# Moving one exp and two value mixing bursts in a fused attention and feed-forward kernel

## The chip, the cores and the metric

The kernel runs on one core of a Trainium2 chip. The metric is the device time of one execution in microseconds; the median of three runs of the kernel before is 246.46 us. A core has TensorE (matrix products into PSUM), VectorE, ScalarE and GpSimd, and queues that issue DMAs; here SyncE issues the outputs and the transposing DMAs, GpSimd the loads.

## The reference

Attention within blocks, where the blocks of keys and values are first mixed by a doubly normalised matrix, and then a gated feed-forward step over all 3072 tokens:

```python
# q, k, v: (4, 8, 768, 64); sort_net: (4, 8, 8, 8); weights 512x1536, 512x1536, 1536x512
P = sort_net
for _ in range(5):
    P = exp(P - max(P, -1)); P = P / (sum(P, -1) + 1e-9); P = P / (sum(P, -2) + 1e-9)
k_sorted = einsum('bhij,bhjcd->bhicd', P, k_b)      # blocks of 96 rows
v_sorted = einsum('bhij,bhjcd->bhicd', P, v_b)
attn = softmax(q_b @ k_sorted.T / 8)                # within each block
x = attn @ v_sorted                                 # as (3072, 512)
g = x @ w_gate
out = (g / (1 + exp(-g)) * (x @ w_val)) @ w_out
```

## The kernel before

After a start-up that computes `P` and the first attention units by hand, the work is written as eight feed-forward passes, `ffn(0)` to `ffn(7)`; the text calls them the first to the eighth pass. Pass `n` takes 384 tokens (half of a batch). It runs 12 steps `m`; each is a `gate` (four matmuls of 128x384, line 410), the tanh on ScalarE (line 418), `gs` on VectorE (line 420), a `value` (four matmuls, line 428) and `h` on VectorE (line 433). `gate` and `value` write to a ring of three PSUM banks ("gen"), so that the third bank after one comes back to it: a `gate` or `value` waits until `gs` or `h` has read what stood there. Between the steps lie the three output steps of the pass before, `outp(n - 1, t3, part)`: three parts of four matmuls (line 445) and, with the last, the copy `o_sb` on ScalarE (line 450) and a DMA from SyncE. In the second pass the output steps come after the steps m = 7, 9 and 11, in the later ones after 3, 7 and 11.

Into these passes `merge` puts the attention of the batches to come. Each side item has a due time; the main items have costs (0.65 for a `gate` or a `value`, 0.87 for an output part), and an item is put behind the first main item at whose end the summed cost has reached its due time. TensorE, GpSimd and ScalarE keep the order in which the program is written; VectorE's order is a planner's.

Attention comes in pairs of units. `scores` writes a unit's scores to one of two wide PSUM tiles, "b" for the first and "a" for the second unit of a pair; `exps` is the exp on ScalarE (line 345); `av` multiplies with the mixed values (line 359), VectorE divides (`r_sb`, line 363, and `st`, line 365), and `x_dma` lets SyncE transpose `st` into `xt`, the next pass's input (line 391). Each of the four `xt` slices of a pass is read by one of a `gate`'s four matmuls. A mixing burst takes the same two wide tiles: `kq_chunk` (keys, line 269) and `v_pair_chunk` (values of batches 2 and 3, line 310) fill "b", which VectorE copies out (line 247), then "a", which ScalarE copies out (line 249). The next burst cannot write a tile before its copy has ended. The values come over `vch`, which GpSimd lays out from a load that a one-element copy, `hold` (line 639), delays until the third pass's input has landed.

Of the kernel before, what the change touches and what calls it, by code (L numbers as in the profile page):

```python
# [17 lines left out]
def kernel(  # L18
# [226 lines left out]
    def drain(eng, dst, src):  # L245
        if eng == "v":
            nc.vector.tensor_copy(dst, src)  # L247
        else:
            nc.scalar.copy(dst, src)  # L249
# [13 lines left out]
    def kq_chunk(b, at, n, eng, tag):  # L263
        dst = kqt_tile(b)[:, 0:2 * GI * C].rearrange("p (n c) -> p n c", c=C)
        rm = rmix[b].rearrange("p a (g two) i -> p two (a g) i", two=2)
        tp = chunk_tile("tkq", n // 8, tag).rearrange("p (l n) -> p l n", n=2 * GI)
        for lc in range(n):
            for two in range(2):
                nc.tensor.matmul(tp[two * D:(two + 1) * D, lc, :],  # L269
                                 lhsT=kq_at(b, at + lc),  # L270
                                 rhs=rm[:, two], start=True, stop=True)
        drain(eng, dst[:, :, at:at + n], tp.transpose([0, 2, 1]))
# [31 lines left out]
    def v_pair_chunk(pair, at, n, eng, tag):  # L304
        dst = vt_tile(pair)[:, :, :, at:at + n]
        tp = chunk_tile("tv", n // 4, tag).rearrange("p (u l n) -> p u l n", u=2, n=H * NB)
        for ld in range(n):
            col = (at + ld) * C
            for u, rows in enumerate((lowr, highr)):
                nc.tensor.matmul(tp[:, u, ld, :], lhsT=vch[rows, col:col + 128],  # L310
                                 rhs=rmix["p"][rows, u].rearrange("p a b -> p (a b)"),
                                 start=True, stop=True)
        drain(eng, dst, tp[0:C].transpose([0, 1, 3, 2]))
# [4 lines left out]
    def scores(b, u, tag):  # L318
        half, g = divmod(u, H2)
        k_sb, k_at, q_sb, q_at = ((kqts[b], 0, kqts[b], GI * C) if b < 2 else  # L320
                                  (kqts["p"], (b - 2) * GI * C, kqts["q"], (b - 2) * GI * C))
        if tag == "gen":
            wide = None
            pss = [bank_tile("qk"), bank_tile("qk")]
        else:
            wide = pair_tile("qk", tag).rearrange("p (two n) -> p two n", two=2)
            pss = [wide[:, 0], wide[:, 1]]
        for i4 in range(4):
            at = (g * NB + half * 4 + i4) * C
            for two in range(2):  # L330
                lo = two * D
                nc.tensor.matmul(pss[two][:, i4 * C:(i4 + 1) * C],  # L332
                                 lhsT=k_sb[lo:lo + D, k_at + at:k_at + at + 128],
                                 rhs=q_sb[lo:lo + D, q_at + at:q_at + at + C],
                                 start=True, stop=True)
        return wide, pss

    def exps(b, u, wide, pss):
        n = ecount[0] % 8
        ecount[0] += 2  # L340
        if wide is None:
            for two in range(2):
                nc.scalar.activation(e_all[:, n + two, 0:4 * C], pss[two][0:C, 0:4 * C], AF.Exp, scale=scale)
        else:
            nc.scalar.activation(e_all[:, n:n + 2, 0:4 * C], wide[0:C, :, 0:4 * C], AF.Exp, scale=scale)  # L345
        es[(b, u)] = [e_all[:, n, :], e_all[:, n + 1, :]]

    def qk(b, u, tag="b"):
        exps(b, u, *scores(b, u, tag))

    def av(b, u, tag="a"):
        half, g = divmod(u, H2)
        vt = vts[b // 2][:, b % 2].rearrange("p (h i) e -> p h i e", h=H)
        av_ps = pair_tile("av_ps", tag).rearrange("p (two n) -> p two n", two=2)
        o = av_ps.rearrange("p two (i e) -> p two i e", i=4)
        for two in range(2):
            e = es[(b, u)][two]
            for i4 in range(4):
                nc.tensor.matmul(o[:, two, i4, 0:D + 1], lhsT=e[:, i4 * C:i4 * C + 128],  # L359
                                 rhs=vt[:, 2 * g + two, half * 4 + i4, 0:D + 1],  # L360
                                 start=True, stop=True)
        r_sb = ssp.tile([C, 2, 4, 1], FP32, name="r_sb", tag="r")
        nc.vector.reciprocal(r_sb, o[0:C, :, :, D:D + 1])  # L363
        st = ssp.tile([C, 4, 2, D], BF16, name="st", tag="st")
        nc.vector.tensor_tensor(st.rearrange("p i two d -> p two i d"), o[0:C, :, :, 0:D],  # L365
                                r_sb.to_broadcast([C, 2, 4, D]), op=ALU.mult)
        sts[(b, u)] = st
# [11 lines left out]
    def xtr(b, u):  # L379
        half, g = divmod(u, H2)  # L380
        if g == 0:
            xts[(b, half)] = xtp.tile([128, H2, TW], BF16, name=f"xt{b}_{half}", tag="xt")
        x_ps = xt_tile("x", 1)[:, 0]
        x_to(x_ps, b, u)
        return xts[(b, half)][:, g, :], x_ps.rearrange("p a b -> p (a b)")

    def x_dma(b, u):
        half, g = divmod(u, H2)
        if g == 0:
            xts[(b, half)] = xtp.tile([128, H2, TW], BF16, name=f"xt{b}_{half}", tag="xt")  # L390
        nc.sync.dma_start_transpose(out=xts[(b, half)][:, g, :].rearrange("p (i c) -> p i c", c=C),
                                    in_=sts.pop((b, u)).rearrange("p i two d -> p (i two d)"))
# [176 lines left out]
    man = tc.manual_schedule(engines={ET.PE, ET.Pool, ET.Activation})  # L569
    man.__enter__()  # L570

    def units(b, us, ats, avs=(1.9, 3.6), lag=3.1):
        us = list(us)
        todo = []
        for n, at in enumerate(ats):
            u, u2 = us[2 * n:2 * n + 2]
            held = []
            todo.append((at, lambda u=u, u2=u2, held=held: (qk(b, u, "b"), held.append(scores(b, u2, "a")))))
            todo.append((at + 1.3, lambda u2=u2, held=held: exps(b, u2, *held[0])))
            for w, tag, t in ((u, "b", avs[0]), (u2, "a", avs[1])):  # L580
                if b == 0:
                    todo.append((at + t, lambda w=w, tag=tag: av(b, w, tag)))
                    todo.append((at + t + lag, lambda w=w: drain("v", *xtr(b, w))))
                else:
                    todo.append((at + t, lambda w=w, tag=tag: (av(b, w, tag), x_dma(b, w))))
        return todo

    def kqs(b, ats):
        return [(at, lambda n=n: (kq_chunk(b, n * 32, 16, "v", "b"), kq_chunk(b, n * 32 + 16, 16, "s", "a")))
                for n, at in enumerate(ats)]  # L590
# [4 lines left out]
    def v_pairs(ats):  # L595
        return [(at, lambda m=m: (v_pair_chunk(1, m * 16, 8, "v", "b"), v_pair_chunk(1, m * 16 + 8, 8, "s", "a")))
                for m, at in ats]

    def merge(main, side):
        done, k = 0.0, 0  # L600
        side = sorted(side, key=lambda t: t[0])
        for c, f in main:
            f()
            done += c
            while k < len(side) and side[k][0] <= done:
                side[k][1]()
                k += 1
        while k < len(side):
            side[k][1]()
            k += 1  # L610

    def ffn(n):
        todo = []
        for m in range(NFC):
            if n > 0 or m > 1:
                todo.append((0.65, lambda m=m: gate(n, m)))
            if n > 0 or m > 0:
                todo.append((0.65, lambda m=m: value(n, m)))
            ends = (7, 9, 11) if n == 1 else (3, 7, 11)
            if n > 0 and m in ends:  # L620
                for part in range(3):
                    todo.append((0.87, lambda t3=ends.index(m), part=part: outp(n - 1, t3, part)))
        return todo
# [7 lines left out]
    def q0_rest():  # L631
        q0_chunk(1, 0, 16, "s", "b")
        q0_chunk(1, 16, 8, "v", "a")

    merge(ffn(0), [(0.0, q0_rest)] + units(0, range(4, 8), (2.0, 6.6)))
    merge(ffn(1), kqs(1, (0.6, 3.3, 7.1)) + vs(v_chunk, 16, (5.2, 5.8, 8.4, 9.1))
          + units(1, range(4), (11.0, 15.6), (1.3, 2.6)))
    hold = const.tile([1, 1], BF16)
    nc.gpsimd.tensor_copy(hold, xts[(1, 0)][0:1, H2 - 1, 0:1])
    load_v(2, 0, 4)  # L640
# [1 line left out]
    for s in range(4):  # L642
        copy_v(nc.gpsimd, 1, both, s)
    nc.vector.memset(kqt_tile("p")[:, 2 * GI * C:], 0.0)
    merge(ffn(2), units(1, range(4, 8), (0.0, 5.5)) + kqs("p", (13.0, 14.7, 20.7)) + v_pairs([(0, 22.5)])
          + [(13.0, lambda: q_dma(2)), (16.4, lambda: q_dma(3))])
    merge(ffn(3), v_pairs([(1, 0.0), (2, 5.1), (3, 6.9)]) + units(2, range(4), (9.8, 14.9)))
    merge(ffn(4), units(2, range(4, 8), (0.0, 8.0)))
    merge(ffn(5), units(3, range(4), (0.0, 8.0)))
    merge(ffn(6), units(3, range(4, 8), (0.0, 8.0)))  # L650
# [36 lines left out]
```

## Time and profile before

| | |
|---|---|
| median of three runs | 246.46 us (246.25 to 246.61) |
| profiled execution | 246.0 us, span 244.2 us |
| TensorE busy | 237.1 us, 97% |
| VectorE busy | 154.8 us, 63% |
| ScalarE busy | 112.3 us, 46% |
| GpSimd busy | 51.3 us, 21% |
| DMA | 24.77 MB, mean 101 GB/s |
| granted TensorE clock | 1.0 |

The span is the time from the first to the last event that the profiler saw; the profiled execution's own time is 1.8 us longer. Lines such as L410 are those of the kernel before. The chain of waits follows the work back from the last instruction, at each step to what released it. "issue" is time in which an engine waited for nothing that the profile shows. PEld is TensorE's loading of weights, which overlaps its matmuls, and SPq is SyncE's queue of DMAs. Where a row has a time and a length, the first number is the start in us from the span's start, the second the length; the modelled ends of matmuls overlap the next ones by a little.

### The profile page before, as it was taken

The numbers are of one execution on the slowest core, as the hardware profiler recorded it, in microseconds if no ns is written. First come the engines' busy times: TensorE is split into PE (matmuls) and PEld (weight loads), VectorE is DVE, ScalarE is ACT, GpSimd is POOL, SyncE is SP. The second block draws the span as 40 slices with busy tenths as digits, with TensorE's granted clock in tenths as the row PEclk, the third lists the DMA queues.
The fourth block names the chain that finished last, engine by engine and source line by source line (L and its number), as shares of the span: only waits on it lengthen the run. The fifth ranks groups of instructions, "written<-read, shape, count | busy, mean of one in ns | idle before, by whom it ended". The sixth has DMA issues, their size and how long they took to land.

```text
span 244.2 us, 6162 instructions
## 1 busy us (share of the span) xinstructions
PE 237.1 (97%) x2617; PEld 139.4 (57%) x2617; DVE 154.8 (63%) x326; ACT 112.3 (46%) x189; POOL 51.3 (21%) x45
## 2 busy tenths in 40 slices
PE   7799999999999999999999999999999999999994
PEld 6375666676455565555555555565556555555543
DVE  6786789876664685777755845674675576445700
ACT  3977554467435435365543452254325334332312
POOL 5992139990002059200000000000000000000000
PEclk9999999999999999999999999999999999999999
DMA  5989999999996999410121212012111211110122
GB/s 99 215 129 208 206 213 213 204 214 190 161 137 139 190 162 159 119 43 3 46 75 32 62 59 71 8 59 63 32 43 46 75 36 43 43 43 3 43 86 86
DMA packets 39642, 24.77 MB, mean 101 GB/s; under 512 B 29376, under 2 KB 34368, under 8 KB 39616
## 3 DMA queue, kind: packets, MB, share of 16 engines
q0 software_dynamic: 19632, 14.16, 38.9%
q1 hardware_dynamic: 19840, 10.17, 17.0%
q8 instruction: 20, 0.33, 0.6%
q10 hardware_dynamic: 144, 0.07, 0.1%
q14 instruction: 6, 0.05, 0.1%
HBM read 28.32 MB, written 7.86 MB: 148 GB/s over the span
## 4 chain that ended last, share of the span: by engine, by line
PE 90%; DVE 4%; DMA 2%; ACT 1%; issue 1%; POOLq 0%
PE v_ps L428 25%; PE o_ps L445 25%; PE g_ps L410 25%; PE av_ps L359 3%; PE qk L332 3%; PE tkq L269 3%; DMA v<-in_v_dram 2%; PE o_ps L461 1%; PE idle_ps L477 1%; PE tv L300 1%; DVE st L365 1%; DVE vt L247 1%; PE tq L279 1%; PE tv L310 1%; PE g_ps L550 1%
## 5 line engine op out<-in xcount | busy, mean ns | idle before, releaser
L420 DVE SCALAR_TENSOR_TENSOR gs_sb<-th_sb,g_ps 128x384 bf16<-128x384 bf16 x96 | 52.9, 551 | 52.4 <-ACT th_sb L418 49.6
L428 PE MATMUL v_ps<-xt,wv_sb 128*128 128x384 bf16 x380 | 77.3, 326 | 0.0
L410 PE MATMUL g_ps<-xt,wg_sb 128*128 128x384 bf16 x376 | 76.6, 325 | 0.2
L418 ACT ACTIVATE th_sb<-g_ps 128x384 bf16<-128x384 f32 x96 | 47.1, 491 | 55.5 <-PE g_ps L410 52.7
L445 PE MATMUL o_ps<-wo,h 128*128 128x512 bf16 x276 | 64.2, 379 | 0.0
L433 DVE SCALAR_TENSOR_TENSOR h<-v_ps,gs_sb 128x384 bf16<-128x384 f32 x96 | 53.4, 556 | 7.6 <-PE tkq L269 0.5
L428 PEld LDWEIGHTS <-wv_sb 128*128 128x128 bf16 x380 | 35.3, 97 | 23.2 <-issue 0.2
L410 PEld LDWEIGHTS <-wg_sb 128*128 128x128 bf16 x376 | 34.9, 97 | 23.7 <-issue 0.4
L445 PEld LDWEIGHTS <-h 128*128 128x128 bf16 x276 | 26.1, 98 | 28.7
L450 ACT COPY o_sb<-o_ps 128x512 f32<-128x512 f32 x23 | 13.5, 586 | 49.0 <-PE o_ps L445 49.0
L148 POOL COPY vch<-v 64x1536 bf16<-64x1536 bf16 (+2 forms) x11 | 28.8, 2657 | 13.0 <-DMA v<-in_v_dram 12.9
L345 ACT ACTIVATE e_all<-qk 96x768 bf16<-96x768 f32 x30 | 23.3, 801 | 4.5 <-PE qk L332 4.5
L365 DVE TENSOR_TENSOR st<-av_ps,r_sb 96x512 bf16<-96x512 f32 x32 | 21.8, 680 | 0.3
L359 PEld LDWEIGHTS <-e_all 96*128 96x128 bf16 x256 | 11.8, 97 | 6.0 <-ACT e_all L345 1.7
L359 PE MATMUL av_ps<-vt,e_all 96*128 96x65 bf16 x256 | 13.1, 193 | 0.5 <-ACT e_all L345 0.5
L249 ACT CAST vt<-tv 96x1024 bf16<-96x1024 f32 (+1 forms) x11 | 10.1, 931 | 4.7 <-PE tv L310 3.6
L363 DVE RECIPROCAL r_sb<-av_ps 96x8 f32<-96x8 f32 x32 | 6.4, 199 | 8.7 <-PE av_ps L359 8.7
L247 DVE CAST vt<-tv 96x1024 bf16<-96x1024 f32 (+1 forms) x7 | 7.4, 1064 | 2.2 <-PE tv L310 1.7
L477 PE MATMUL idle_ps<-warm_sb 128*128 128x512 bf16 x25 | 7.6, 411 | 0.0
L247 DVE COPY oq_v<-o_ps 128x128 f32<-128x128 f32 x1 | 0.3, 292 | 9.3 <-PE o_ps L461 9.3
L395 POOL DMA_DIRECT2D q_scr<-in_q_dram x2 | 5.6, 3178 | 0.0
L146 ACT COPY vch<-v 64x768 bf16<-64x768 bf16 (+1 forms) x4 | 5.4, 1384 | 0.2 <-DMA v<-in_v_dram 0.2
(83 smaller groups left out, 129.8 us busy)
## 6 DMA issues: line engine op xcount, KB each, us to landing
out_dram<-o_sb SPq DMA_DIRECT2D x23, 256.0 KB, 2.0
v<-in_v_dram POOLq DMA_DIRECT2D x4, 384.0 KB, 12.6
wg_sb<-in_moe_w_gate_dram POOLq DMA_DIRECT2D x3, 512.0 KB, 11.2
wv_sb<-in_moe_w_val_dram POOLq DMA_DIRECT2D x3, 512.0 KB, 13.0
wo<-in_moe_w_out_dram POOLq DMA_DIRECT2D x3, 512.0 KB, 16.2
kqp<-in_k_dram POOLq DMA_DIRECT2D x2, 768.0 KB, 10.1
q_scr<-in_q_dram POOLq DMA_DIRECT2D x2, 768.0 KB, 18.8
v<-in_v_dram POOLq DMA_DIRECT2D x2, 768.0 KB, 9.8
```

The source lines that it names most:

```text
L148: eng.tensor_copy(dst, src.transpose([0, 2, 1]))
L247: nc.vector.tensor_copy(dst, src)
L345: nc.scalar.activation(e_all[:, n:n + 2, 0:4 * C], wide[0:C, :, 0:4 * C], AF.Exp, scale=scale)
L359: nc.tensor.matmul(o[:, two, i4, 0:D + 1], lhsT=e[:, i4 * C:i4 * C + 128], rhs=vt[:, 2 * g + two, half * 4 + i4, 0:D + 1], start=True, sto ...
L365: nc.vector.tensor_tensor(st.rearrange("p i two d -> p two i d"), o[0:C, :, :, 0:D], r_sb.to_broadcast([C, 2, 4, D]), op=ALU.mult)
L410: nc.tensor.matmul(g_ps, lhsT=wg_sb[:, kc, ts(m, 128)], rhs=xt[:, kc, :], start=(kc == 0), stop=(kc == NKC - 1))
L418: nc.scalar.activation(th_sb, g_ps, AF.Tanh, scale=0.5)
L420: nc.vector.scalar_tensor_tensor(gs_sb, th_sb, 1.0, g_ps, op0=ALU.add, op1=ALU.mult)
L428: nc.tensor.matmul(v_ps, lhsT=wv_sb[:, kc, ts(m, 128)], rhs=xt[:, kc, :], start=(kc == 0), stop=(kc == NKC - 1))
L433: nc.vector.scalar_tensor_tensor(h_tiles[n][:, m, :], v_ps, 0.5, gs_tiles.pop(m), op0=ALU.mult, op1=ALU.mult)
L445: nc.tensor.matmul(o_ps, lhsT=h_w[:, m, ts(t3, 128)], rhs=wo_sb[part][:, m % 4, :], start=(m == 0), stop=(m == NFC - 1))
L450: nc.scalar.copy(o_sb, o_ps)
```

## The change

`units` gets a parameter for the time between a pair's scores and its second exp; it was 1.3 and stays so everywhere but in the second pass, where it is 0.9. In the third pass the first value mixing burst is due at 21.6 instead of 22.5, and the second, which was the first side item of the fourth pass, is due at 22.5 in the third.

```diff
-    def units(b, us, ats, avs=(1.9, 3.6), lag=3.1):
+    def units(b, us, ats, avs=(1.9, 3.6), lag=3.1, second=1.3):
...
             todo.append((at, lambda u=u, u2=u2, held=held: (qk(b, u, "b"), held.append(scores(b, u2, "a")))))
-            todo.append((at + 1.3, lambda u2=u2, held=held: exps(b, u2, *held[0])))
+            todo.append((at + second, lambda u2=u2, held=held: exps(b, u2, *held[0])))
...
     merge(ffn(1), kqs(1, (0.6, 3.3, 7.1)) + vs(v_chunk, 16, (5.2, 5.8, 8.4, 9.1))
-          + units(1, range(4), (11.0, 15.6), (1.3, 2.6)))
+          + units(1, range(4), (11.0, 15.6), (1.3, 2.6), second=0.9))
...
-    merge(ffn(2), units(1, range(4, 8), (0.0, 5.5)) + kqs("p", (13.0, 14.7, 20.7)) + v_pairs([(0, 22.5)])
+    merge(ffn(2), units(1, range(4, 8), (0.0, 5.5)) + kqs("p", (13.0, 14.7, 20.7)) + v_pairs([(0, 21.6), (1, 22.5)])
           + [(13.0, lambda: q_dma(2)), (16.4, lambda: q_dma(3))])
-    merge(ffn(3), v_pairs([(1, 0.0), (2, 5.1), (3, 6.9)]) + units(2, range(4), (9.8, 14.9)))
+    merge(ffn(3), v_pairs([(2, 5.1), (3, 6.9)]) + units(2, range(4), (9.8, 14.9)))
```

On ScalarE the second exp of the second pass's first pair comes to stand ahead of the copy of the first output step. On TensorE the last output step of the third pass reads: last key burst, part one, first value burst, part two, second value burst, part three, and then the fourth pass's first `gate`; before, it read key burst, parts one and two, first value burst, part three, `gate`, second value burst, `value`. The order on SyncE and GpSimd is the same in both kernels.

## Prediction

> **What bounds the kernel.** I read the page first (busy times, then the chain of waits), then the table of waits of TensorE, then the chain and the timeline in the two stretches that the diff touches, and last the times to landing of the DMAs that those stretches start.
>
> ```profile
> PE 237.1 (97%) x2617; PEld 139.4 (57%) x2617; DVE 154.8 (63%) x326; ACT 112.3 (46%) x189; POOL 51.3 (21%) x45
> PE 90%; DVE 4%; DMA 2%; ACT 1%; issue 1%; POOLq 0%
> PE av_ps L359 <- ACT e_all L345: 0.5, 1, 0.5
> ```
>
> TensorE is busy 97% of the span and is 90% of the chain that ended last. After the start-up it waits by name for another engine once in the whole run: 0.5 us for an exp. A change of order can therefore gain only where TensorE stands still, and costs wherever it makes TensorE stand still anew. The named wait lies in the second pass (chain of waits, that stretch; start, us, what):
>
> ```profile
> 62.38 0.26 PE av_ps L359 x8
> 62.90 0.82 ACT e_all L345
> 63.76 0.42 PE av_ps L359 x8
> 64.18 0.65 PE v_ps L428 x4
> ```
>
> TensorE's timeline gives `gate` at 62.46 and the next `value` at 64.02; between them stands the second `av` of the pair, held until ScalarE has finished its exp. ScalarE's rows there are: exp of the first unit 60.42 to 61.23, idle 1.19, copy `o_sb` 62.42 to 63.01, exp of the second unit 62.90 to 63.71. The second exp had its scores long before: it stood behind a copy that itself waited for TensorE.
>
> The other stretch is the seam between the third and fourth pass (timeline; idle time before an instruction in brackets):
>
> ```profile
> 101.56 1.22 DVE L247 CAST kqtp<-tkq 128x1024 bf16<-128x1024 f32 x1
> 101.61 1.90 PE L445 MATMUL o_ps<-wo,h 128*128 128x512 bf16 x8
> 103.44 0.64 PE L310 MATMUL tv<-rmixp,vch 64*128 64x64 bf16 x32
> 103.89 1.22 DVE L247 CAST vt<-tv 96x1024 bf16<-96x1024 f32 x1 [1.11 <-PE tv L310]
> 104.12 1.01 ACT L249 CAST vt<-tv 96x1024 bf16<-96x1024 f32 x1 [1.39 <-PE tv L310]
> 105.64 0.64 PE L310 MATMUL tv<-rmixp,vch 64*128 64x64 bf16 x32
> 106.73 1.21 DVE L247 CAST vt<-tv 96x1024 bf16<-96x1024 f32 x1
> 107.87 0.54 DVE L433 SCALAR_TENSOR_TENSOR h<-v_ps,gs_sb 128x384 bf16<-128x384 f32 x1
> 108.46 0.81 PE L410 MATMUL g_ps<-xt,wg_sb 128*128 128x384 bf16 x4
> ```
>
> The first mixing burst (103.44) finds its PSUM tile long free. The second (105.64) sends a cast to VectorE ahead of `h`; `h` ends at 108.41, and the `gate` that needs the bank it frees starts at 108.46 instead of 108.17 (0.65 after the `value` at 107.52). That is a hold of 0.29 us which the table of waits does not name.
>
> **Edit 1, the exp.** In the second pass the first pair's second exp now stands right behind the first exp, ahead of the copy. For the second pair of that pass the new due time (16.5 instead of 16.9) falls behind the same output part as before, so nothing moves there. No instruction is added. The two exps run as one stretch of 1.50 us (the second pair's row at 66.45), so the second ends at about 61.9, before the copy's data is there at 62.4: the copy costs nothing more, it lies in the idle 1.19. The `av` then starts as the matching place in the third pass does (`gate` 84.46, `value`, then `av` 85.76 and `gate` 86.01): 0.65 for the `gate`, 0.25 for the `av`. From `gate` to `value` that is 0.90 instead of 64.02 - 62.46 = 1.56. **Gain 0.66, taken as 0.65** (the start of the `av` moves from 63.76 to 63.11).
>
> What is late next: VectorE now does reciprocal, `gs`, `st`, `h` from 63.6 on, by the spacing of its rows at 64.12 to 65.43 ending `h` at about 65.6; the output step that takes the bank of that `value` comes at 66.51 - 0.65 = 65.86, so 0.3 remains. SyncE's transposes of this unit and the two later ones are issued earlier by the same shift; the queue order of SyncE and GpSimd does not change.
>
> **Edit 2, the bursts.** Of the third pass's last output step (three parts of four matmuls), the first burst moves from behind part two to behind part one, the second from behind the next pass's first `gate` to behind part two. TensorE's work is the same; four changes between burst and other work before, four after. The cover of each PSUM drain shrinks. Step by step, in the old times:
> - The drain of the last key burst ends at 101.56 + 1.22 = 102.78. Part one starts at 101.61 and is over for the next burst after about 0.96 (half of 1.83, plus the change), 102.57. First burst at 102.82: **held 0.25**.
> - From a burst's start to its VectorE cast 0.45 (103.44 to 103.89), cast 1.22, release 0.04: 1.71. Under it lie the burst (0.57, 103.44 to 104.02) and one part (0.96): 1.53. Second burst at 104.53: **held 0.18**.
> - Second burst 0.57, part three 0.87 (104.02 to 104.89): first `gate` at 105.97. ScalarE's casts (1.01 each, 0.68 behind the bursts) end at 106.22, when the copy of the output wants to start anyway. From first to third `gate` an undisturbed pass takes 2.64 (95.12 to 97.76): third `gate` at 108.61 instead of 108.46.
>
> **Sum of edit 2: 0.15 later, taken as 0.14** (the next burst at 111.19 comes out 0.14 later): the hold of 0.29 and its side effects go, 0.43 come. Bounds: below, -0.29, if only the old hold goes and both drains happen to end in time; above, +0.54, if the key drain ends as late after its burst as the first key burst's (90.14 to 92.85, 2.71 instead of 2.31, 0.40 more). I take the middle rows, since they are those of this very place.
>
> **Total: -0.65 + 0.14 = -0.51.** The profiled execution took 246.0 (span 244.2 and 1.8 around it), so 245.5 for it; its time is 0.46 below the median of the runs, 246.46. On the median: 245.95. A measurement of this kernel can tell about 0.2%, 0.49 us, from no change: the forecast lies on that edge.
>
> **A rule against it.** The four transposes that make the next pass's input are on their way while GpSimd's cast of q still occupies the DMA engines; to landing they take 7.7, 7.1, 3.9 and 2.3 us (issues at 63.62, 66.05, 69.65, 72.61), faster as that traffic ends. The fourth lands by 74.99, when GpSimd's `hold` copy that waits for it runs; the `gate` at 74.83 needs it for its fourth matmul, at 75.32. So 0.33 of cover is all there is.
> The Trainium skill, DMA: Bandwidth & Descriptors, section "Issuing engines are not separate DMA queues", says that DMAs of different issuing engines share the same 16 engines and interleave; read strictly, issuing earlier only queues earlier, and the sum would be that of rival B below.
>
> A second one: TensorE's granted clock stayed at 1.00 through both holds (windows of 2 and 10 us; TensorE's busy time first).
>
> ```profile
> 62.00:64.00 2.00, 1.51 (x22) 0.87 (x21) 0.89 (x2) 1.58 (x3) 0.00 (x0) 1.00 2.48 157
> 100.00:110.00 10.00, 9.87 (x170) 5.76 (x168) 7.14 (x11) 5.44 (x8) 0.00 (x0) 1.00 0.12 47
> ```
>
> The Trainium skill, TensorE: Matmul & The Clock Gate, section "A second HAM failure mode: psum-queue depth-cycling", warns that short idles while PSUM banks are cycled can throttle the clock; one 3.4 us window at half clock, an estimate from that page, would make the total about +1.2. The 0.65 hold above did not do it, so I give that no place in the sum.
>
> **Rivals.**
> - **B, the fourth transpose does not move.** The output DMA ahead of it on SyncE took 1.68 us to issue (70.87) where others take 0.33 to 0.54, as if held by what was still under way. If its landing stays at 74.99 while the matmul wants it at 74.67, TensorE waits 0.32: -0.51 + 0.32 = -0.19, 246.27. Against it: all that the fourth transpose waits for (its `st`, the output copy) moves with TensorE.
> - **C, slower.** The fourth transpose meets more of the q traffic and takes 3.9 like the third: issued at 71.96 it lands at 75.86, 1.19 after its matmul wants it: -0.51 + 1.19 = +0.68, 247.14. It decides against the change from a landing of 3.7 on (a wait of 1.0). Against it: at 72 to 73 us the DMA share was down to 0.06.
> - **D, the bursts cost nothing.** -0.65 - 0.29 = -0.94, 245.52. For it: VectorE is better placed after the seam, with both casts out of the way of `gs` and `h`. Against it: the drain of 1.22 is longer than one part.
> - That the exp does not change its place is excluded by the order on ScalarE, which has the two exps together.
>
> **How the numbers follow.** A 0.50, B 0.28, C 0.12, D 0.10. A's own range, by the bounds of edit 2, is 245.5 to 246.35; two thirds of its weight lie below 245.97. Faster: 0.33 of A, 0.10 of D, 0.05 of B (cheap bursts): 0.48. Slower: C 0.12 and 0.02 from the dear ends of A and B: 0.14. Same: 0.38. The range goes from D (245.52, less a little for the spread of the runs, 246.25 to 246.61) to B with the dear end of edit 2 (-0.65 + 0.32 + 0.54 = +0.21, 246.67): 245.45 to 246.65, which leaves out C and the tails.
>
> **What would show it.** In the profile of the changed kernel: no wait of `av` for the exp; from the second pass's ninth `value` on, everything 0.65 earlier; the first `gate` of the third pass without a gap between its third and fourth matmul (a gap there is B or C, its length says which); the first burst held about 0.25 and the second about 0.18, both ended by VectorE's casts; no hold at the third `gate` of the fourth pass; the burst after that at 111.19 - 0.51 = 110.7. The prediction is wrong if a named wait remains in the second pass, if the seam costs over 0.5, or if the shift at 111 us is not the shift at the end.

## The result and the profile after

The changed kernel has a median of 245.52 us (245.47 to 245.80, seven runs) beside 246.46 us of the kernel before (246.05 to 246.88, seven runs): ratio 0.9968, 95% interval 0.9957 to 0.9978. In a later comparison it was 245.60 beside 246.11, ratio 0.9978 (0.9968 to 0.9988). The forecast was 245.95, -0.51; the second comparison gives -0.51, the first -0.94. The profiled execution took 245.8, span 244.0, only 0.2 less than the profiled one of before, so the two traces alone do not show the gain of the runs; the steps have to be read one by one.

The page, lines one and four's head:

```profile
PE 238.3 (98%) x2617; PEld 139.8 (57%) x2617; DVE 154.9 (63%) x326; ACT 112.4 (46%) x189; POOL 51.2 (21%) x45
PE 91%; DVE 6%; DMA 1%; ACT 1%; issue 0%; DVEq 0%
```

TensorE has 1.2 us more counted as busy. That is not more work: it runs 2617 matmuls in both, and 1.1 of the 1.2 lies between 5 and 10 us, in warm-up matmuls of the start-up, the same 17 in both. The start-up is 0.10 later in this one (the second pass's first `av` at 62.32 instead of 62.22). All differences below are taken from that point on.

The stretch of the exp (chain of waits; start, us, what):

```profile
62.73 0.65 PE g_ps L410 x4
63.38 0.24 PE av_ps L359 x8
63.62 0.65 PE v_ps L428 x4
```

No exp stands in the chain any more, and the named wait of `av` is gone from TensorE's table. The two exps now run as one stretch ahead of the copy (timeline of ScalarE):

```profile
60.52 1.50 ACT L345 ACTIVATE e_all<-qk 96x768 bf16<-96x768 f32 x2 [1.05 <-PE qk L332]
```

On TensorE's timeline, from `gate` (62.56) to `value` (63.46) it is 0.90, as forecast. Before it was 1.56 (timeline of the kernel before):

```profile
62.46 0.81 PE L410 MATMUL g_ps<-xt,wg_sb 128*128 128x384 bf16 x4
64.02 0.81 PE L428 MATMUL v_ps<-xt,wv_sb 128*128 128x384 bf16 x4
```

The first `gate` of the third pass, 0.66 ahead of the old time when the 0.10 is taken off, does not run through (chain of waits):

```profile
74.43 0.49 PE g_ps L410 x3
74.92 0.03 issue
74.95 0.32 PE g_ps L410
```

Three matmuls run, and the fourth starts at 74.95. The timeline gives the whole `gate` 1.00 where 0.81 is usual, so the fourth is 0.19 late. The reason is on SyncE's queue (timeline; start, us, engine, line, what), where the output DMA now takes 2.20 to issue and the fourth transpose stands behind it, and on GpSimd, whose `hold` copy marks the landing:

```profile
74.27 1.00 PE L410 MATMUL g_ps<-xt,wg_sb 128*128 128x384 bf16 x4
70.31 2.20 SPq L452 DMA_DIRECT2D out_dram<-o_sb  x1
72.56 1.20 SPq L391 DMA_TRANSPOSE xt<-st  x1
74.96 0.18 POOL L639 COPY hold<-xt 1x1 bf16<-1x1 bf16 x1 [19.59 <-DMA xt<-st]
```

The same two in the kernel before:

```profile
72.61 1.21 SPq L391 DMA_TRANSPOSE xt<-st  x1
74.99 0.18 POOL L639 COPY hold<-xt 1x1 bf16<-1x1 bf16 x1 [20.35 <-DMA xt<-st]
```

Both stayed where they were, although TensorE's work ahead of them came 0.56 earlier on this trace's clock (0.66 less the 0.10 of the start-up).

The seam of the third and fourth pass (timeline):

```profile
100.10 1.20 PE L269 MATMUL tkq<-rmixp,kqp 128*64 128x64 bf16 x64
101.19 1.22 DVE L247 CAST kqtp<-tkq 128x1024 bf16<-128x1024 f32 x1
102.45 0.64 PE L310 MATMUL tv<-rmixp,vch 64*128 64x64 bf16 x32 [0.18 <-DVE kqtp L247]
102.90 1.22 DVE L247 CAST vt<-tv 96x1024 bf16<-96x1024 f32 x1 [0.50 <-PE tv L310]
103.03 1.04 PE L445 MATMUL o_ps<-wo,h 128*128 128x512 bf16 x4
104.17 0.64 PE L310 MATMUL tv<-rmixp,vch 64*128 64x64 bf16 x32
104.62 1.22 DVE L247 CAST vt<-tv 96x1024 bf16<-96x1024 f32 x1 [0.50 <-PE tv L310]
105.62 0.81 PE L410 MATMUL g_ps<-xt,wg_sb 128*128 128x384 bf16 x4
110.99 0.64 PE L310 MATMUL tv<-rmixp,vch 64*128 64x64 bf16 x32
```

Each burst starts 0.04 to 0.05 after the VectorE cast before it ends (102.41 and 104.12). Part one starts at 101.23 and would be over for the burst at 102.19; it is held 0.26. (The holds are reckoned from the starts, with 0.96 for a part; the view in brackets counts idle time only from the modelled end of the matmul before, and so shows less, 0.18 for the first and nothing for the second.) Part two starts at 103.03; the second burst is held 0.18. The third `gate` at 108.27 is not held. From the key burst (100.10) to the third value burst (110.99) it is 10.89. Before it was 10.71 (timeline of the kernel before):

```profile
100.48 1.20 PE L269 MATMUL tkq<-rmixp,kqp 128*64 128x64 bf16 x64
111.19 0.64 PE L310 MATMUL tv<-rmixp,vch 64*128 64x64 bf16 x32
```

So the seam costs 0.18.

### The profile page after: what moved, and what is told of

It reads as the page before. It is cut to its first block, busy times and chain, and to the rows that moved or that the text cites. A ratio compares the mean times of both kernels' runs of the same rounds, so it can differ in the third digit from the quotient of the medians.

```text
span 244.0 us, 6162 instructions
## 1 busy us (share of the span) xinstructions
PE 238.3 (98%) x2617; PEld 139.8 (57%) x2617; DVE 154.9 (63%) x326; ACT 112.4 (46%) x189; POOL 51.2 (21%) x45
## 4 chain that ended last, share of the span: by engine, by line
PE 91%; DVE 6%; DMA 1%; ACT 1%; issue 0%; DVEq 0%
PE v_ps L428 25%; PE g_ps L410 25%; PE o_ps L445 24%; PE av_ps L359 3%; PE qk L332 3%; PE idle_ps L477 2%; PE tkq L269 2%; DVE vt L247 1%; PE o_ps L461 1%; PE tv L300 1%; PE tv L310 1%; DVE st L365 1%; PE tq L279 1%; DMA p_sb<-in_sort_net_dram 1%; PE g_ps L550 1%; DVE kqt L247 1%
## 5 line engine op out<-in xcount | busy, mean ns | idle before, releaser
L477 PE MATMUL idle_ps<-warm_sb 128*128 128x512 bf16 x25 | 9.2, 487 | 0.0
```

The lines of the kernel that those rows point to most:

```text
L477: nc.tensor.matmul(tile, lhsT=warm_sb[:, 0:128], rhs=warm_sb, start=True, stop=True)
```

## The experiments

Each kernel was timed 5 to 12 times; the kernels of one chip are compared with the kernel before on that chip. Seam means the time from the last key burst to the third value burst.

| kernel | median | before, same chip | ratio (95%) | seam | wait at the `gate` of 74 us |
|---|---|---|---|---|---|
| before, again | 246.19 | 246.11 | 1.0005 (0.9996 to 1.0014) | 10.70 | 0 |
| exp only | 245.45 | 246.11 | 0.9982 (0.9959 to 1.0005) | 10.71 | 0 |
| bursts only | 246.40 | 246.11 | 1.0010 (0.9999 to 1.0021) | 10.89 | 0.88 |
| changed, again | 245.60 | 246.11 | 0.9978 (0.9968 to 0.9988) | 10.88 | 0.08 |
| changed, output DMA on GpSimd | 245.83 | 246.23 | 0.9984 (0.9975 to 0.9993) | 10.88 | 0 |
| exp, output DMA on GpSimd | 245.73 | 246.23 | 0.9986 (0.9975 to 0.9997) | 10.71 | 0 |
| bursts back to back | 246.22 | 246.23 | 1.0006 (0.9996 to 1.0016) | 11.50 | 0.05 |
| exp, second burst later | 245.35 | 246.23 | 0.9968 (0.9956 to 0.9980) | 10.70 | 0 |
| before, q cast late | 246.10 | 246.07 | 1.0001 (0.9992 to 1.0010) | 10.71 | 0 |
| changed, q cast late | 245.58 | 246.07 | 0.9977 (0.9968 to 0.9986) | 10.88 | 0 |
| exp, q cast late | 245.40 | 246.07 | 0.9970 (0.9959 to 0.9981) | 10.71 | 0 |
| exp and first burst | 245.70 | 246.07 | 0.9980 (0.9969 to 0.9991) | 10.96 | 0.08 |

The last column is the time from the start of the third pass's first `gate` to the start of what follows it, less 0.75, the time that this takes in the kernel before (74.83 to 75.58). Seam and wait are read from one profiled execution of each kernel.

**The kernel before, again** (no edit).

> The kernel before, unchanged, for a second profile. The profile of before had a time of 246.0, the lowest of its eight; that of the changed kernel 245.8, the highest of its seven. Theory T1 (the two profiles show the change as it is, +0.18 at the seam, -0.48 at the exp, -0.30 together, and the runs' larger gap is spread): a second profile has the same hold of 0.65 at the av of the second pass and of 0.29 at the gate of the seam, with nothing else, and the median lies near 246.2. Theory T2 (the first profile was of an unusually quick execution of the kernel before, and most executions lose some 0.5 more at a place that the change removes or that it does not touch): the second profile shows that place, as a hold of TensorE of 0.2 to 0.6 that the first one does not have, and the median lies near 246.5.

The second profile repeats the first: the `av` 0.49 idle, the third `gate` of the seam at 108.47, span 244.2. Its time is 246.02, its runs 245.98 to 246.84. So both profiles are of shorter executions of this kernel, and where the longer ones lose is in neither.

**The exp alone.**

```diff
-          + units(1, range(4), (11.0, 15.6), (1.3, 2.6)))
+          + units(1, range(4), (11.0, 15.6), (1.3, 2.6), second=0.9))
```

> Only the second exp is moved ahead of the copy; the bursts stay. T1: the av starts 0.65 earlier, the first gate of the third pass waits 0.2 for its fourth transpose, so -0.48 against the kernel before, ratio about 0.998, and the seam keeps its hold of 0.29. T2, the extra loss at the seam of the kernel before: also -0.48 to -0.65. T3, the extra loss lies at the exp or at the transposes: -0.9 or more, ratio 0.9965 or below, as much as the whole change.

-0.66 on the medians; its interval is wide because one of its twelve runs took 248.85, the others 245.17 to 245.63. What that one run lost is not shown. From `gate` to `value` 0.89. In this execution the fourth transpose was issued at 70.77 and landed by 74.06: no wait, so all 0.65 came through. The seam keeps 10.71 with its hold of 0.29 at the third `gate`.

**The bursts alone.**

```diff
-    merge(ffn(2), ... + v_pairs([(0, 22.5)])
+    merge(ffn(2), ... + v_pairs([(0, 21.6), (1, 22.5)])
...
-    merge(ffn(3), v_pairs([(1, 0.0), (2, 5.1), (3, 6.9)]) + ...
+    merge(ffn(3), v_pairs([(2, 5.1), (3, 6.9)]) + ...
```

> Only the two value mixing bursts are moved; the exp stays behind the copy. T1: +0.18 (holds of 0.26 and 0.18 at the bursts instead of 0.29 at the gate), ratio about 1.0007. T2 (the kernel before usually loses more at the seam than its first profile shows): -0.2 to -0.5, ratio 0.998 to 0.999. T3 (extra loss at the exp or the transposes): +0.18 like T1.

+0.29 on the medians, so the bursts alone do not help; the interval takes in T1's +0.18 and leaves out T2's gains. Its profiled execution took 247.13, its longest, and shows a loss much larger than in any other profile (table of waits, timeline of TensorE, timeline of SyncE):

```profile
PE g_ps L410 <- DMA xt<-st: 0.7, 1, 0.7
76.26 0.32 PE L410 MATMUL g_ps<-xt,wg_sb 128*128 128x384 bf16 x1 [0.73 <-DMA xt<-st]
69.69 3.53 SPq L391 DMA_TRANSPOSE xt<-st  x1
73.27 0.58 SPq L452 DMA_DIRECT2D out_dram<-o_sb  x1
73.89 1.22 SPq L391 DMA_TRANSPOSE xt<-st  x1
```

The third transpose, 1.18 in the profiles of before and after, took 3.53 to issue; the fourth went out at 73.89, landed 2.3 later as before, and the `gate`'s fourth matmul ran at 76.26. (The table of waits names 0.73; by the starts it is 0.88.) Up to 100 us this program is the kernel before, unchanged, so the kernel before is open to the same loss, though neither of its two profiles shows it.

**The changed kernel, again** (no edit).

> The changed kernel, for a second profile. T1: the first profile's picture: waits of 0.26 and 0.18 at the bursts, 0.19 at the fourth matmul of the third pass's first gate, span about 244.0. T2 and T3: the first profile was of a slow execution of the changed kernel (245.8 where the others are 245.5): the second has a span of 243.7, and the 0.3 between them lies at the fourth transpose (no wait there) or before 60 us, where the first one was 0.10 later than the kernel before.

Span 243.9, `hold` at 74.81 instead of 74.96, `gate` wait 0.08 instead of 0.19: of the 0.15 by which this execution is ahead at the third value burst (110.84 for 110.99), 0.11 is this wait and 0.04 the start-up.

**One output DMA on GpSimd**, with the change and with the exp alone.

```diff
-        nc.sync.dma_start(out=out[ds(base, 128), :], in_=o_sb)
+        queue = nc.gpsimd if (n, t3) == (0, 1) else nc.sync
+        queue.dma_start(out=out[ds(base, 128), :], in_=o_sb)
```

> The changed kernel, with one output DMA (first pass's tokens, second output step, the one that stands on SyncE's queue between the third and fourth transpose of the third pass's input) issued from GpSimd's queue, which is idle then. In the two profiles of the changed kernel SyncE spent 2.20 and 2.06 on issuing it and the fourth transpose landed 0.14 to 0.2 too late; with only the bursts moved the third transpose took 3.53 to issue and TensorE waited 0.73. Theory Q (SyncE's queue is held there until the q cast's traffic has ended, and the fourth transpose is late only because it stands behind): the fourth transpose is issued at about 70.2, lands before 74.2, no wait at the first gate of the third pass, 0.1 to 0.2 less than the changed kernel (245.3 to 245.4, ratio 0.997) and a narrower spread of the runs. Rival (the transpose itself moves only when the traffic has ended): landing at 74.8 to 75.0 as before, same time as the changed kernel.

> Only the exp moved, bursts as before, and the same output DMA on GpSimd's queue. Theory Q with the seam as read (+0.18 for the bursts): the best of all, -0.65 to -0.7 against the kernel before, 0.18 less than the changed kernel with the same DMA moved; no slow runs like the 0.7 wait. Rival (transpose not helped): like the exp alone, ratio 0.998, with runs up to 0.5 longer among them.

Half of theory Q held. In the changed kernel `hold` ran at 74.31 and the `gate` was not held. But the transpose was not issued quickly either: third and fourth together took 3.97 from 69.10 on, so the queue was slow for whatever stood there. And the times did not fall, nor did the runs lie closer together: against the kernel before on the same chip the gain is 0.40 with the change and 0.50 with the exp alone, where it was 0.51 and 0.66 without this edit; the intervals overlap. The executions are 2.1 longer than their spans in the median of the 22 runs of these two kernels (246.01 and 243.9, 245.67 and 243.6 in the profiled ones), where the others are 1.8: what was saved inside the span was spent around it. Why a DMA issued from GpSimd costs that is not shown here.

**Bursts back to back.**

```diff
-    ... v_pairs([(0, 21.6), (1, 22.5)])
+    ... v_pairs([(0, 22.5), (1, 22.5)])
```

> The changed kernel, but both bursts behind part two of the output step, with no matmuls between them. If a burst is held by the VectorE cast of the one before (1.71 from a burst's start to its tile free), the second waits 1.71 - 0.57 = 1.14, the first gate follows part three, and the third gate of the pass comes 0.77 later than with the exp alone: about -0.65 + 0.77 = +0.1 against the kernel before, 0.6 more than the changed kernel. If the casts were not what holds the bursts (weight loads or changes of matmul shape instead), it costs nothing against the changed kernel.

Its timeline names the hold:

```profile
104.57 0.64 PE L310 MATMUL tv<-rmixp,vch 64*128 64x64 bf16 x32 [1.08 <-DVE vt L247]
```

1.72 after the first burst's start (102.85), as reckoned (1.71), and the seam is 11.50: +0.79 against the exp alone, where +0.77 was expected. The time, 246.22, is level with the kernel before: the whole gain of the exp is eaten. So the VectorE cast is what holds a burst, and the matmuls between two bursts are its cover. ScalarE's cast ends at nearly the same moment (104.54), but it frees the tile that only the second half of the next burst writes.

**The second burst later.**

```diff
-    merge(ffn(3), v_pairs([(1, 0.0), (2, 5.1), (3, 6.9)]) + ...
+    merge(ffn(3), v_pairs([(1, 1.3), (2, 5.1), (3, 6.9)]) + ...
```

> Only the exp moved; the second burst stays in the fourth pass but comes behind its first value instead of ahead of it, and VectorE's order then has h ahead of the cast. If the hold of 0.29 is only a matter of that order, it goes: 0.29 less than with the exp alone (ratio 0.997 against the kernel before). If VectorE has no room there (gs and h take 1.32 a step, TensorE's gate and value 1.30), the cast delays the next gs, and the third value is held 0.27 instead: same as the exp alone.

The second reading held (timeline, VectorE and TensorE):

```profile
107.01 1.21 DVE L247 CAST vt<-tv 96x1024 bf16<-96x1024 f32 x1
108.14 0.54 DVE L420 SCALAR_TENSOR_TENSOR gs_sb<-th_sb,g_ps 128x384 bf16<-128x384 bf16 x1
108.73 0.81 PE L428 MATMUL v_ps<-xt,wv_sb 128*128 128x384 bf16 x4
```

`h` is out ahead of the cast, but the next `gs` is not; the `value` that follows the `gate` of 107.79 starts at 108.73 instead of 108.44, held 0.29. The seam is 10.70, as with the exp alone: the hold changed its owner. Its median is the lowest of all, within 0.1 of the exp alone on two other chips. Against the kernel before on its own chip it is -0.88, where the exp alone has -0.66 and, with the q cast late, -0.67; with five runs, and with intervals that overlap, it can't be told from the exp alone.

**The q cast out of the way**, in the kernel before, the changed one and the exp alone.

```diff
     q_cast(2)
-    q_cast(3)
...
     for s in range(4):
         copy_v(nc.gpsimd, 1, both, s)
+    q_cast(3)
...
-          + [(13.0, lambda: q_dma(2)), (16.4, lambda: q_dma(3))])
+          + [(13.0, lambda: q_dma(2))])
...
-    merge(ffn(4), units(2, range(4, 8), (0.0, 8.0)))
+    merge(ffn(4), units(2, range(4, 8), (0.0, 8.0)) + [(12.0, lambda: q_dma(3))])
```

> The kernel before, with the second of the two q casts (768 KB read, GpSimd's queue, 52 to 72 us) issued behind the value layout copies of the same queue, after 99 us, and its transposing load later with it. The transposes of the third pass's input then meet no such traffic. Theory Q (what varies from run to run, 245.8 to 247.1 in the kernel before, is the landing of the fourth of these transposes against the gate that needs it): all four transposes land in about 2.4, the runs lie within 0.3 of each other near the lowest of the kernel before (245.9 to 246.1). Rival (the spread comes from the start-up or from elsewhere): same spread as before.

> The changed kernel with the same q cast moved. Theory Q: no wait at the first gate of the third pass, so the change is worth just its two edits, -0.65 + 0.18 = -0.47 against the kernel before with the cast moved, and 0.1 to 0.2 less than the changed kernel: near 245.4. Rival: same as the changed kernel, and spread as there.

> Only the exp moved, with the same q cast moved: -0.65 against the kernel before with the cast moved, 0.18 less than the changed kernel with the cast moved; the best so far at 245.2 to 245.3 if theory Q holds, with no run above 245.6.

In the kernel before the four transposes now land in 2.5, 2.3, 2.3 and 2.3 (7.7, 7.1, 3.9, 2.3 with the cast there), and the runs lie between 246.01 and 246.32. In the changed kernel the first q cast, which kept its place, was still under way until about 66 us; there the first two transposes took 4.5 and 3.5, the last two 2.3. With the cast in its old place 21 of the 98 runs of the kernel before, over four sets, lie above 246.45, up to 247.07. The eleven runs of the kernel before here have none of these, but eleven are few. Over all kernels with the cast in its old place 30 of 200 runs lie more than 0.35 above the median of their set; of the 28 runs of the three kernels here none does. Together with the long execution of the bursts alone, whose trace has the wait, this speaks for the cast as the source of the longer executions. It is not shown run by run, since no long execution of the kernel before was profiled. In the changed kernel (SyncE and GpSimd, timeline):

```profile
70.30 0.58 SPq L452 DMA_DIRECT2D out_dram<-o_sb  x1
70.92 1.19 SPq L391 DMA_TRANSPOSE xt<-st  x1
73.31 0.18 POOL L638 COPY hold<-xt 1x1 bf16<-1x1 bf16 x1 [18.68 <-DMA xt<-st]
```

The output DMA issues in 0.58 instead of 2.20, the landing is 1.65 earlier, the `gate` is not held. Between kernels that all have the cast late the change is worth 245.58 - 246.10 = -0.52, the exp alone 245.40 - 246.10 = -0.70.

**The exp and the first burst.**

```diff
-    ... v_pairs([(0, 21.6), (1, 22.5)])
+    ... v_pairs([(0, 21.6)])
...
-    merge(ffn(3), v_pairs([(2, 5.1), (3, 6.9)]) + ...
+    merge(ffn(3), v_pairs([(1, 0.0), (2, 5.1), (3, 6.9)]) + ...
```

> The exp moved, and of the two bursts only the first (behind part one); the second stays behind the fourth pass's first gate. By the steps of the prediction the first burst is held 0.26 by the key drain, nothing is saved at the gate, where the hold of 0.29 stays: 0.26 more than with the exp alone, 0.08 more than the changed kernel. If the first burst's place is what frees VectorE after the seam, the hold of 0.29 goes with it and it is equal to the exp alone.

Seam 10.96, +0.25 against the exp alone (0.26 expected) and +0.08 against the changed kernel (0.08 expected). The first burst pays its hold and saves nothing; moving the second as well trades the hold of 0.29 at the `gate` for one of 0.18.

## Why the prediction was right, step by step

- **The exp, -0.65: right.** 0.66 in each profile with the edit, and -0.66 and -0.70 on the medians with it alone. The copy was not delayed (62.52 instead of 62.42, the start-up's 0.10), and `h` ended at 65.55 where 65.6 was reckoned, ahead of the output part that needs its bank (65.95).
- **The bursts, +0.14: right**, +0.17 to +0.18 in every profile with both bursts moved as in the change. The two holds were 0.26 and 0.18 for 0.25 and 0.18; what is left over is 0.03 to 0.04. Case D fell: the old hold went, but two came.
- **The fourth transpose (rival B): right in kind, but given as a case where it is a term.** Its issue stayed at 72.4 to 72.6 in the profiles of the changed kernel; the wait was 0.19 and 0.08, not 0.32, since the start-up put TensorE 0.10 and 0.06 later in these executions and the landing was 0.03 and 0.18 earlier. It did not come at all in the execution with the exp alone, where the output DMA issued in 0.58. The argument against B, that all the fourth transpose waits for moves with TensorE, left out the queue that it is issued from: with its inputs 0.56 earlier, it went out at the old time. The best account of the change is -0.66 + 0.18 + 0 to 0.19.
- **Rival C: not met.** In the two profiles of the changed kernel the fourth transpose took 2.3 and 2.4 to landing, as before. With the exp alone it went out at 70.77 and did take longer, 3.2, as C has it, but it still landed 0.9 earlier than before. The loss of 0.88 at this place was seen in the kernel with only the bursts moved, where the exp is late, and it came another way: through the third transpose's issue of 3.53.
- **What failed: the step that put the profiled time beside the median.** I took the 0.46 between them as a constant to be carried over. It is not one: the same kernel had medians of 246.46, 246.11, 246.23 and 246.07 in four sets, and its profiled executions of 246.0 lie below all of them. The first set, from which the 0.46 came, has the highest median. So 245.95 came out 0.43 too high although the difference of -0.51 was met where the sets were larger. The first set's -0.94 is not explained term by term; four of its seven runs of before lie at 246.46 or above, and the intervals of the two ratios overlap. That 245.52 is the very number of rival D is chance, since D's free bursts did not come. Part of the -0.94 may be a gain that the sum has at nothing: with the cast in its old place and all outputs on SyncE, 22 of 121 runs with the exp behind the copy lie more than 0.35 above the median of their set, and 4 of 57 with the exp ahead of it. Why that should be is not shown.
- **The signs.** The first `gate` of the third pass has the gap that was to be absent, 0.19. The third value burst came at 110.99 where 110.7 was forecast; the 0.3 between them is the start-up's 0.10, this gap and the 0.04 by which the seam was reckoned too cheap. At the end of the span the shift is the same 0.2 as at 111 us.
- **The two rules.** The Trainium skill, DMA: Bandwidth & Descriptors, section "Issuing engines are not separate DMA queues", which says that DMAs of all issuers share 16 engines and interleave, agrees with the runs: in the kernel before SyncE's first two transposes land in 7.7 and 7.1 us beside GpSimd's casts, and in 2.5 and 2.3 with the second cast moved away. What TensorE: Matmul & The Clock Gate, section "A second HAM failure mode: psum-queue depth-cycling", warns of did not happen: the granted clock was 1.00 from 100 to 110 us, both in the changed kernel and in the one with the bursts back to back, where TensorE was busy 8.71 of these 10 us.

The part that brings the gain is the exp alone. It was below the changed kernel in both direct comparisons: 245.45 and 245.60, and 245.40 and 245.58 with the q cast late. These 0.15 and 0.18 are near the 0.17 to 0.18 that the seam costs in the traces, but the intervals of the ratios overlap.

## What to carry to other kernels

On an engine that keeps its order, look at what stands ahead of an operation whose data is ready: an exp behind a copy that waits for the bottleneck engine makes that engine wait for the exp in its turn, here 0.66 us. Before a burst is moved closer to another that shares its PSUM tile, compare the drain's round trip (here 1.71) with the work between them (here 1.53); the difference is the hold. And where a transfer lands 0.3 ahead of its reader, take its spread from several executions before taking the profiled one as typical.

## What the runs showed of the hardware that was not expected

An issue on SyncE's queue can itself be long while a cast from GpSimd's queue loads the DMA engines: the same output DMA took 0.58 to 2.20 and the third transpose 1.18 to 3.53, and what stands behind on the queue is late by that. With the second cast moved away the output DMA took 0.58 in all three profiles, and no transpose of this input more than 1.50. A single output DMA moved to GpSimd's queue did not lengthen the span, but lengthened the execution around it by 0.3 in the median of the runs, in both kernels that had it.
